# Right-hand weights of the last layer: half of the chunks converted straight into their final buffers, half parked in HBM

## The chip, the cores and the metric

One Trainium2 chip, one core. The time is device microseconds of one execution, the median over runs. Engines: PE is TensorE, DVE is VectorE, ACT is ScalarE, POOL is GpSimd, SP is SyncE, which issues nearly all transfers of this kernel.

## The reference

Windowed attention (4 batches, 8 heads, 576 positions, window 64, scaled scores, softmax) gives `x` of 2304 x 512. Then two MLPs of width 2048:

```python
h = x @ w_in
g = np.maximum(h, 0.0) + alpha * np.minimum(h, 0.0)
x = (g @ w_out).astype(np.float32)
...
h = x @ w_in
g = h * (1.0 / (1.0 + np.exp(-h)))
return (g @ w_out).astype(np.float32)
```

The weights of the second MLP are `w_in2` and `w_out2`. All weights come as 64-bit floats.

## The kernel before, in words

The 2304 tokens are 6 tiles of 384. The kernel runs in four layers: attention with the first product of MLP 1, the second product of MLP 1 ("layer 2"), the first of MLP 2 ("layer 3") and the second of MLP 2 ("layer 4"). Layers 2 to 4 do each 2 x 2 block product with seven products in place of eight (a Winograd form of Strassen's scheme), so each needs seven combinations of left sides and seven of right sides. For precision an operand is split into a high part, which ScalarE casts to `fp32r` (line 339), and a remainder, which VectorE subtracts (line 340); `parts` does the cast at once and puts the remainder on the list `lows`, and `rests` issues these at the next step. Three matmuls (high by high, high by remainder, remainder by high) make one product.

Layer 3 has `NU` = 3 thirds (pairs of token tiles, `u`) of `KH` = 8 units each (chunks of 128 columns, `c`), and `unit(u, c, ...)` runs seven products of six matmuls (line 572) in the order B11, T3, B21, T2, T4, B22 of the unit before, T1. After a product ScalarE copies a bank (`fork`, line 577, tile `fk`), VectorE adds (`blend`, line 582, tile `c`), ScalarE applies SiLU and SP stores the tile to HBM (`finish`, lines 587 and 589, tiles `g`). Between two products stands `hook(h)`, h from 0 to 6. It issues the remainders that wait and then whatever the table `plan` holds for `slot(u, c, h) = LAY3 + (u * KH + c) * 7 + h`. `plan` is filled ahead of time: this is where work for layer 4 is placed. `(2, 5, 4)` below stands for slot(2, 5, 4). Everything issued goes to the engines' queues in that order, and each engine takes its queue in order.

Layer 4 has 168 steps `n` (56 for each pair of token tiles); a step is nine matmuls (line 688) on one hidden tile `g` (split by `split_g2`, three steps ahead) and one right side `w`. Hidden tiles come back by `load_g2` (line 643); `sum_g2` makes the left combinations on VectorE (line 663) or by an adding transfer (line 650).

The right sides of layer 4 are made from `w_out2` in 8 chunks of 128 rows and their partners. For a chunk, `park` loads two tiles of 512 KB (`stage`, line 321, tiles `s`, a pool of four buffers), converts 64-bit to 32-bit in three VectorE operations each (`f32_step`, lines 326, 329, 332, tiles `cva`), makes four combinations into one buffer `ts` (`combos`, line 370; the pool `tp` has a single buffer) and writes all seven right sides to HBM (lines 897 to 899, `w_o`). Later `unpark` fetches one right side (128 KB, line 909) and splits it. `job` spreads a chunk's steps evenly from slot w0 to w1 and puts its loads some 9 us ahead, though not before the buffer's last user, which the list `taken` keeps.

Before the change, chunks 0 to 2 are parked in the first third of layer 3 (6 hooks each), 3 to 5 in the second and 6 and 7 in the last (7 each). Of the 56 right sides 37 are fetched in the last third, the other 19 (`late`) in layer 4 from step 12 on, each two steps ahead of its cast. Layer 3's own right sides come in the same way from `w_i`.

Of the kernel before, what the change touches and what calls it, by code (L numbers as in the profile page):

```python
# [8 lines left out]
F32 = mybir.dt.float32  # L9
F32R = mybir.dt.float32r  # L10
# [34 lines left out]
def attention_two_mlps(ctx, tc, q, k, v, w_in1, w_out1, alpha, w_in2, w_out2, out):  # L45
# [43 lines left out]
    def lroom(i, shape, dtype, name):  # L89
        return wroom(HOMES[i % 64], shape, dtype, name)  # L90
# [228 lines left out]
    def stage(src, f):  # L319
        s = stg.tile([P, 2 * DM], U32, name="s64", tag="st")  # L320
        nc.sync.dma_start(out=s, in_=src[f * P:(f + 1) * P, :])
        return s.rearrange("p (f t) -> p f t", t=2)
# [19 lines left out]
    def rests():  # L342
        while lows:
            lows.pop(0)()
# [286 lines left out]
    def load_g2(u, x, c):  # L631
        if u >= NU:
            return
        i, jj, at = {A11: (0, 0, 0), A21: (1, 0, 8), A22: (1, 1, 16), A12: (0, 1, 24)}[x]

        at = (24 - at) if u % 2 and x in (A11, A12) else at
        if u == 0 and x in (A11, A21):

            g = lroom(32 + c if x == A11 else (40, 41, 42, 43, 44, 45, 46, 48)[c], [P, TN], F32, "g")
        else:  # L640
            g = room(at + c, name="g")
        gb[u, x, c] = g
        nc.sync.dma_start(out=g, in_=gd2[2 * u + i, c + KH * jj])

    def sum_g2(u, x, c):
        if u >= NU:
            return

        def add(a, b):
            nc.gpsimd.dma_start(out=gb[u, a, c], in_=gb[u, b, c], accum_op=ALU.add)  # L650
            gb[u, x, c] = gb[u, a, c]
        if x == S4:
            return add(S2, A12)
        if x == S1 and u:
            return add(A21, A22)
        a, b, op = {S3: (A11, A21, ALU.subtract), S1: (A21, A22, ALU.add), S2: (S3, A22, ALU.subtract)}[x]
        if x == S3:
            o = lroom(24 + c if u == 0 and c < 3 else 48 + c, [P, TN], F32, "s3")
        elif u == 0:
            o = room(c if x == S2 else 8 + c, name="s")  # L660
        else:
            o = gb[u, A11, c]
        nc.vector.tensor_tensor(out=o, in0=gb[u, a, c], in1=gb[u, b, c], op=op)
        gb[u, x, c] = o
# [204 lines left out]
    def park(key, c, src, w0, w1):  # L869

        def load(i):
            held.setdefault((key, c), []).append(stage(src, c + i * KH))

        a = {}

        def convert(i, k):
            if k == 0:
                a[i] = cv.tile([P, DM], U32, name="cva", tag="cv")
            f32_step(held[key, c][i], a[i], k)

        def combine(k):
            x, y = (a[i].bitcast(F32) for i in range(2))
            if k == 0:
                a[2] = tp.tile([P, 4, HD], F32, name="ts", tag="ts")
            t = a[2]
            if key == "i2":
                combos(x[:, :HD], y[:, :HD], x[:, HD:], y[:, HD:], t, k)
            else:
                combos(x[:, :HD], x[:, HD:], y[:, :HD], y[:, HD:], t, k, minus=True)
            if k < 3:  # L890
                return
            d = dram.tile([P, 7, HD], F32, name=f"w2_{key}_{c}")
# [12 lines left out]
    def unpark(key, c, v, to):  # L905
# [7 lines left out]
            parts(s[:, 1, :].bitcast(F32), s[:, 0, :], s[:, 1, :])  # L913
        return fetch, split

    def rights3(c, w0, w1):

        for i, v in enumerate(PARKED):
            g = w0 + i * (w1 - w0) // 7
            fetch, split = unpark("i2", c, v, 7 * c + i)  # L920
            at(g - 10, fetch)
            at(g, split)

    def left_sides(u, places, loads_at):
# [6 lines left out]

        taken.extend((places[7], places[9], places[8], places[10]))

    g = -62
    for x in "0 1 a 2 3 b 4 5 c 6 7 d e".split():
        if x.isdigit():
# [8 lines left out]
                      (5, slot(0, 1, 4), slot(0, 3, 1)), (6, slot(0, 3, 1), slot(0, 4, 4)), (7, slot(0, 4, 4), slot(0, 6, 0))):  # L945
        rights3(c, w0, w1)
    left_sides(0, (147, 149, 150, 151, 153, 157, 159, 161, 163, 165, 167), [138, 139, 140, 141])
    g = LAY3 + 9
    for c in range(3):
        park("o2", c, w_out2, g + 6 * c, g + 6 * c + 6)  # L950
    for u in range(NU - 1):
        left_sides(u + 1, [slot(u, c, h) for c, h in ((5, 5), (6, 0), (6, 1), (6, 3), (6, 5), (7, 2), (7, 3), (7, 4), (7, 5), (8, 0), (8, 6))],
                   [slot(u, 4, h) for h in range(3, 7)])
        g = slot(u + 1, 0, 3) + (4 if u == 0 else 6)
        for c in ((3, 4, 5), (6, 7))[u]:
            park("o2", c, w_out2, g, g + 7)
# [3 lines left out]
    order = [m for m in range(7 * KH) if m not in late]  # L960
    order = [m for m in order if m not in (6, 7, 14, 15, 22, 23)]
    order[20:20] = [6, 7, 14, 15, 22, 23]
    for i, m in enumerate(order):
        plan.setdefault(slot(2, 0, 3) + i * 9 // 8, []).append(rights[m][0])
        plan.setdefault(slot(2, 1, 0) + i * 9 // 8, []).append(rights[m][1])

    def hook(g):
        rests()
# [56 lines left out]
    after1.pop(0)()  # L1025
    put_x2()

    for i, c in enumerate(range(KH)):
        at(slot(2, 6, 1) + i * 3 // 4, lambda c=c: load_g2(0, A11, c))
        at(slot(2, 6, 6) + i * 3 // 4, lambda i=i: load_g2(0, A21, i))  # L1030
    for i in range(3):
        if i < 2:
            at(slot(2, 7, 4) + i, lambda i=i: split_g2(i))
        at(slot(2, 7, 2) + i, lambda i=i: sum_g2(0, S3, i))

    prev = None
    for u in range(NU):
# [4 lines left out]
    split_g2(2)  # L1042
    for n in range(NU * STEPS):
        rests()
        if n == 2:
            last_product(prev, stg.tile([P, TN], F32, name="c", tag="st"))
            for c in range(KH):
                load_g2(0, A22, c)
        split_g2(n + 3)
        around2(n)  # L1050
        if n < 5:
            sum_g2(0, S3, 3 + n)
        for i, m in enumerate(late):
            if n == 14 + i * 30 // len(late):
                rights[m][1]()

        if n % KH == 3:
            while ready:
                ready.pop(0)()
        step2(n)  # L1060
        for i, m in enumerate(late):
            if n == 12 + i * 30 // len(late):
                rights[m][0]()


# [45 lines left out]
```

## Time and profile before

| | before |
|---|---|
| median of 3 runs | 835.59 us (834.38 to 836.41) |
| the profiled execution | 840.68 us |
| its span | 838.9 us |
| TensorE busy | 809.0 us (96% of the span) |
| VectorE, ScalarE, GpSimd busy | 631.8, 523.0, 79.9 us |
| granted TensorE clock, mean | 0.994 |
| moved by DMA | 190.47 MB |

Times in the rows below count from the start of the span. A clock of 1.00 is the higher of TensorE's two levels, 2.4 GHz. The chain follows the work that ended last backwards, at each step to what released it; where it says PE for many pieces, nothing else held the end up there. Layer 3 begins at 464.93 us.

### The profile page before, as it was taken

To read this page: it belongs to the slowest core of one execution; us is meant where nothing else is said; L and a number is where in the kernel's file an instruction comes from. 1 tells how busy PE (TensorE), PEld (TensorE's weight loads), DVE (VectorE), ACT (ScalarE), POOL (GpSimd) and SP (SyncE) were. 2 spreads that over 40 slices of the span, in tenths; PEclk is the share of its full clock that TensorE was granted. 3 is DMA by queue.
4 is the path that set the end of the run, shared out by engine and by line. 5 is a ranking of instruction groups with operands and counts; after the bars stand their busy time and mean duration, and the time that the engine had idled before them with its cause. 6 is when DMAs were issued, how large, how long until landed. Compare 5 with 4: busy or idle time off the path is not lost.

```text
span 838.9 us, 17786 instructions
## 1 busy us (share of the span) xinstructions
PE 809.0 (96%) x5976; PEld 786.7 (94%) x5976; DVE 631.8 (75%) x1593; ACT 523.0 (62%) x1381; POOL 79.9 (10%) x108
## 2 busy tenths in 40 slices
PE   5899999999999999999999989999999999999998
PEld 4789999899899999999999989999899999999998
DVE  6897458888988999887889775756664877756754
ACT  6997696676655776554577556546565564554543
POOL 1000000000000033122222000000000020321400
PEclk9999999999999999999999999999999999999999
DMA  8792468788585899999997786784788879659621
GB/s 274 227 312 104 160 197 273 227 291 260 182 290 183 285 212 225 297 227 264 314 240 202 242 313 217 246 304 157 261 271 268 262 167 326 136 120 307 120 59 57
DMA packets 136844, 190.47 MB, mean 227 GB/s; under 512 B 13872, under 2 KB 122928, under 8 KB 136752
## 3 DMA queue, kind: packets, MB, share of 16 engines
q1 hardware_dynamic: 124080, 172.02, 62.4%
q0 software_dynamic: 12672, 17.31, 12.5%
q8 instruction: 47, 0.77, 0.4%
q14 instruction: 45, 0.37, 0.2%
HBM read 110.11 MB, written 61.87 MB: 205 GB/s over the span
## 4 chain that ended last, share of the span: by engine, by line
PE 79%; DMA 9%; DVE 7%; ACT 3%; issue 1%; SPq 1%; ACTq 0%; DVEq 0%
PE acc L688 20%; PE acc L493 19%; PE h L391 18%; PE qa L572 10%; PE qd L572 5%; DMA w<-w_o 3%; PE qb L572 2%; DMA s<-in_moe_w_in_dram 2%; PE pa L293 2%; PE pa L272 2%; PE pa L206 1%; DMA g<-g 1%; DMA kT<-in_k_dram 1%; ACT pr L229 1%; DMA alpha_sb<-in_moe_alpha_dram 1%
## 5 line engine op out<-in xcount | busy, mean ns | idle before, releaser
L391 PE MATMUL h<-x,i 128*128 128x384 f32 x1152 | 210.0, 339 | 2.1 <-DVE i L365 1.2
L391 PEld LDWEIGHTS h<-x,i 128*128 128x128 f32 x1152 | 199.8, 189 | 5.6 <-ACT g L399 2.4
L688 PE MATMUL acc<-w,gh 128*128 128x256 f32 x984 | 145.7, 283 | 0.4 <-ACT gh L339 0.3
L493 PE MATMUL acc<-gh,o 128*128 128x384 f32 x672 | 143.7, 334 | 0.6 <-ACT gh L339 0.6
L688 PEld LDWEIGHTS acc<-w,gh 128*128 128x128 f32 x984 | 130.3, 192 | 1.1 <-ACT gh L339 1.1
L339 ACT CAST gh<-gf 128x384 fp32r<-128x384 f32 x168 | 85.6, 515 | 57.6 <-PE acc L493 48.3
L493 PEld LDWEIGHTS acc<-gh,o 128*128 128x128 f32 x672 | 118.9, 188 | 0.9 <-ACT gh L339 0.9
L572 PE MATMUL qa<-v,w 128*128 128x384 f32 x576 | 110.5, 339 | 5.5 <-ACT fk L577 3.9
L572 PEld LDWEIGHTS qa<-v,w 128*128 128x128 f32 x576 | 101.8, 190 | 7.2 <-ACT fk L577 5.2
L340 DVE TENSOR_TENSOR gl<-gf,gh 128x384 fp32r<-128x384 f32 x168 | 91.7, 557 | 15.8 <-ACT gh L339 12.2
L339 ACT CAST gh<-g 128x384 fp32r<-128x384 f32 x116 | 58.3, 514 | 48.0 <-PE acc L688 46.9
L688 PE MATMUL acc<-w,gl 128*128 128x256 f32 x492 | 86.7, 283 | 0.0
L493 PE MATMUL acc<-gl,o 128*128 128x384 f32 x336 | 86.0, 336 | 0.3 <-DVE gl L340 0.2
L340 DVE TENSOR_TENSOR gl<-g,gh 128x384 fp32r<-128x384 f32 x116 | 62.8, 556 | 29.7 <-ACT gh L339 28.6
L398 ACT ACTIVATE a<-h 128x384 f32<-128x384 f32 x96 | 47.1, 490 | 56.8 <-PE h L391 47.6
L452 POOL DMA_DIRECT2D gf<-gf x48 | 42.0, 909 | 403.6 <-DVE o L340 298.3
L413 DVE SCALAR_TENSOR_TENSOR g<-a,nalpha,g 128x384 f32<-128x384 f32 x96 | 59.0, 615 | 23.3 <-ACT g L399 22.0
L688 PEld LDWEIGHTS acc<-w,gl 128*128 128x128 f32 x492 | 71.3, 192 | 0.0
L340 DVE TENSOR_TENSOR w<-w 128x256 fp32r<-128x256 f32 x112 | 46.7, 422 | 22.6 <-ACT w L339 22.2
L493 PEld LDWEIGHTS acc<-gl,o 128*128 128x128 f32 x336 | 60.2, 188 | 2.3 <-DVE gl L340 2.2
L229 ACT ACTIVATE pr<-pr,nm 128x128 f32<-128x128 f32 x144 | 56.1, 395 | 8.7 <-DVE nm L217 8.7
L339 ACT CAST w<-w 128x256 fp32r<-128x256 f32 x112 | 43.5, 402 | 24.7 <-DMA w<-w_o 20.4
(90 smaller groups left out, 1121.3 us busy)
## 6 DMA issues: line engine op xcount, KB each, us to landing
g<-g SPq DMA_DIRECT2D x192, 192.0 KB, 4.2
gf<-g SPq DMA_DIRECT2D x96, 192.0 KB, 4.2
g<-c SPq DMA_DIRECT2D x96, 192.0 KB, 3.0
s<-in_moe_w_in_dram SPq DMA_DIRECT2D x32, 512.0 KB, 5.9
s<-in_moe_w_out_dram SPq DMA_DIRECT2D x32, 512.0 KB, 5.8
gf<-gf POOLq DMA_DIRECT2D x48, 192.0 KB, 5.3
w<-w_i SPq DMA_DIRECT2D x56, 128.0 KB, 4.1
w<-w_o SPq DMA_DIRECT2D x56, 128.0 KB, 3.3
```

Of the source, the lines that this page charges most:

```text
L229: nc.scalar.activation(out=pr[:, j, :], in_=pr[:, j, :], func=AF.Exp, bias=it[f"nm{hf}"][:, j:j + 1], scale=-1.0, accum_out=it["sm"][:, hf ...
L272: nc.tensor.transpose(pb[:, j * P:(j + 1) * P], it[f"p{hf}"][:, j, :], ident)
L293: nc.tensor.matmul(pb[r, jb * W:(jb + 1) * W], vt[:, jb // 2, r], it[f"pt{hf}"][:, j, side(jb, e)], start=True, stop=True)
L339: nc.scalar.copy(hi, src)
L340: lows.append(lambda: nc.vector.tensor_tensor(out=lo, in0=src, in1=hi.bitcast(F32), op=ALU.subtract))
L391: nc.tensor.matmul(h, w[:, kk, :], x, start=(kk == 0 and n == 0), stop=(kk == KD - 1 and n == 2))
L398: nc.scalar.activation(out=a, in_=h, func=AF.Relu, scale=-1.0)
L413: nc.vector.scalar_tensor_tensor(out=g, in0=a, scalar=nalpha[:, f:f + 1], in1=g, op0=ALU.mult, op1=ALU.add)
L452: nc.gpsimd.dma_start(out=o, in_=g1[u, b, c], accum_op=ALU.add)
L493: nc.tensor.matmul(o[i], w[:, a, i * P:(i + 1) * P], b, start=start and a == 0 and b is gh, stop=c == KH - 1 and b is gl, skip_group_check ...
L572: nc.tensor.matmul(o, w[:, a, k0], b, start=start and kk == 0 and n == 0, stop=kk == 1 and n == 2, skip_group_check=True)
L688: nc.tensor.matmul(acc2[u, v][i], a[:, i * P:(i + 1) * P], w[:, b, :], start=v in (A11, A12, S3) and c == 0 and a is gh and b == 0 and i != 1,
```

## The change

Chunk 0 alone is parked in the first third, over 14 hooks; chunks 1, 2 and 3 in the second, 9 hooks each. Chunks 7, 6, 5 and 4 are no longer parked: `direct` loads, converts and combines them in the last third and splits the seven results straight into the buffers from which layer 4 reads them. These are places that layer 3's own right sides have left by then. Only the 28 right sides of chunks 0 to 3 are fetched: 8 in the last third, 20 in layer 4 from step 5 on, each five steps ahead of its cast. The first tiles of layer 4 (`A11` and `A21`) are loaded in turn from (2, 5, 4) on, and the next ones (`A22`) partly before layer 4 begins. Some tiles get other places.

```diff
-            g = lroom(32 + c if x == A11 else (40, 41, 42, 43, 44, 45, 46, 48)[c], [P, TN], F32, "g")
+            g = lroom(((28, 29, 31, 32, 33, 34, 35, 30) if x == A11 else (40, 39, 36, 41, 38, 42, 37, 43))[c], [P, TN], F32, "g")
...
-            o = lroom(24 + c if u == 0 and c < 3 else 48 + c, [P, TN], F32, "s3")
+            o = lroom((47, 46, 45, 48, 49, 54, 50, 53)[c], [P, TN], F32, "s3")
...
+    def direct(c, w0, w1, to):
+
+        key, a = ("o2", c), {}
+
+        def load(i):
+            held.setdefault(key, []).append(stage(w_out2, c + i * KH))
+
+        def convert(i, k):
+            if k == 0:
+                a[i] = cv.tile([P, DM], U32, name="cva", tag="cv")
+            f32_step(held[key][i], a[i], k)
+
+        def combine(k):
+            x, y = (a[i].bitcast(F32) for i in range(2))
+            if k == 0:
+                a[2] = tp.tile([P, 4, HD], F32, name="ts", tag="ts")
+            combos(x[:, :HD], x[:, HD:], y[:, :HD], y[:, HD:], a[2], k, minus=True)
+
+        def split(i):
+            s = wt["o2", c, PARKED[i]] = lroom(to + i, [P, 2, HD], F32R, "w2")
+            src = a[2][:, i - 3, :] if i > 2 else a[(i + 1) // 2].bitcast(F32)[:, HD * (i == 2):HD * (i == 2) + HD]
+            parts(src, s[:, 0, :], s[:, 1, :])
+        job([lambda: load(0), lambda: load(1)], CONVERT(convert) + [lambda k=k: combine(k) for k in range(4)] +
+            [lambda i=i: split(i) for i in (0, 5, 1, 4, 6, 2, 3)], w0, w1, 6)
...
-    g = LAY3 + 9
-    for c in range(3):
-        park("o2", c, w_out2, g + 6 * c, g + 6 * c + 6)
...
-        g = slot(u + 1, 0, 3) + (4 if u == 0 else 6)
-        for c in ((3, 4, 5), (6, 7))[u]:
-            park("o2", c, w_out2, g, g + 7)
-            g += 7
-    rights = [unpark("o2", m % KH, SEQ[m // KH], 56 + m) for m in range(7 * KH)]
-    late = list(range(4 * KH, 4 * KH + 3)) + list(range(5 * KH, 7 * KH))
...
-        plan.setdefault(slot(2, 0, 3) + i * 9 // 8, []).append(rights[m][0])
-        plan.setdefault(slot(2, 1, 0) + i * 9 // 8, []).append(rights[m][1])
+    park("o2", 0, w_out2, LAY3 + 15, LAY3 + 29)
+    left_sides(1, LEFT(0), [slot(0, 4, h) for h in range(3, 7)])
+    for c in (1, 2, 3):
+        park("o2", c, w_out2, slot(1, 0, 3) + 9 * (c - 1), slot(1, 0, 3) + 9 * c)
+    left_sides(2, LEFT(1), [slot(1, 4, h) for h in range(3, 7)])
+    direct(7, slot(2, 0, 4), slot(2, 1, 6), 56)
+    direct(6, slot(2, 1, 6), slot(2, 3, 0), 0)
+    direct(5, slot(2, 3, 0), slot(2, 4, 2), 7)
+    direct(4, slot(2, 4, 2), slot(2, 5, 4), 14)
+    SPOTS = [63, *range(21, 28), 44, 55, 51, 52, *range(28, 36), *range(36, 44)]
+    rights = [unpark("o2", m % KH, SEQ[m // KH], SPOTS[j]) for j, m in
+              enumerate(KH * k + c for k in range(7) for c in range(4))]
+    for j in range(8):
+        at(slot(2, 4, 6) + 3 * j // 2, rights[j][0])
+        at(slot(2, 5, 6) + 3 * j // 2, rights[j][1])
...
-        at(slot(2, 6, 1) + i * 3 // 4, lambda c=c: load_g2(0, A11, c))
-        at(slot(2, 6, 6) + i * 3 // 4, lambda i=i: load_g2(0, A21, i))
+    for c in range(KH):
+        for x in (A11, A21):
+            at(slot(2, 5, 4) + (2 * c + (x == A21)) * 7 // 8, lambda c=c, x=x: load_g2(0, x, c))
...
-        at(slot(2, 7, 2) + i, lambda i=i: sum_g2(0, S3, i))
+        at(slot(2, 7, 3) + i, lambda i=i: sum_g2(0, S3, i))
+    for c in range(4):
+        at(slot(2, 7, 5) + c // 2, lambda c=c: load_g2(0, A22, c))
...
+        if n < 2:
+            for c in (4 + 2 * n, 5 + 2 * n):
+                load_g2(0, A22, c)
         if n == 2:
             last_product(prev, stg.tile([P, TN], F32, name="c", tag="st"))
-            for c in range(KH):
-                load_g2(0, A22, c)
...
-            if n == 14 + i * 30 // len(late):
-                rights[m][1]()
+        for j in range(8, len(rights)):
+            if n == 10 + (j - 8) * 3 // 2:
+                rights[j][1]()
...
-            if n == 12 + i * 30 // len(late):
-                rights[m][0]()
+        for j in range(8, len(rights)):
+            if n == 5 + (j - 8) * 3 // 2:
+                rights[j][0]()
```

Three places show how the rows move. In them `w_...` are right sides (those split from themselves were fetched), `s_...` the loaded 64-bit tiles, `cva` the converted ones.

The first is VectorE in the first third of layer 3, between the blend of `qd` in unit 2 and the blend of `qb` in unit 3. Before:

```order
L582 TENSOR_TENSOR c<-qd,fk 128x384
L340 TENSOR_TENSOR w_6872<-w_6872 128x256
L332 SCALAR_TENSOR_TENSOR cva<-s_6855,cva 128x512
L370 TENSOR_TENSOR ts<-cva 128x256
L340 TENSOR_TENSOR w_6886<-w_6886 128x256
L370 TENSOR_TENSOR ts<-cva 128x256
L370 TENSOR_TENSOR ts<-ts,cva 128x256
L370 TENSOR_TENSOR ts<-cva,ts 128x256
L582 TENSOR_TENSOR c<-qa,fk 128x384
L340 TENSOR_TENSOR w_6913<-w_6913 128x256
L326 TENSOR_SCALAR cva<-s_6947 128x512
L326 TENSOR_SCALAR cva<-s_6949 128x512
```

Now:

```order
L582 TENSOR_TENSOR c<-qd,fk 128x384
L340 TENSOR_TENSOR w_6868<-w_6868 128x256
L340 TENSOR_TENSOR w_6882<-w_6882 128x256
L329 SCALAR_TENSOR_TENSOR cva<-s_6851,cva 128x512
L332 SCALAR_TENSOR_TENSOR cva<-s_6849,cva 128x512
L582 TENSOR_TENSOR c<-qa,fk 128x384
L340 TENSOR_TENSOR w_6905<-w_6905 128x256
L332 SCALAR_TENSOR_TENSOR cva<-s_6851,cva 128x512
```

The second parked chunk's combinations stood between the two blends, with a third chunk behind; now the only chunk of this third is still being converted there.

The second is VectorE in the last third, around the blend of `qa` in unit 2. Before (the parking of chunk 6 and the remainders of fetched right sides):

```order
L340 TENSOR_TENSOR w_8359<-w_8359 128x256
L370 TENSOR_TENSOR ts<-cva 128x256 x2
L582 TENSOR_TENSOR c<-qa,fk 128x384
L340 TENSOR_TENSOR w_8375<-w_8375 128x256
L370 TENSOR_TENSOR ts<-ts,cva 128x256
L340 TENSOR_TENSOR w_8391<-w_8391 128x256
L370 TENSOR_TENSOR ts<-cva,ts 128x256
L582 TENSOR_TENSOR c<-qb,fk 128x384
```

Now (chunk 6 by `direct`):

```order
L329 SCALAR_TENSOR_TENSOR cva<-s_8253,cva 128x512
L582 TENSOR_TENSOR c<-qa,fk 128x384
L329 SCALAR_TENSOR_TENSOR cva<-s_8284,cva 128x512
L332 SCALAR_TENSOR_TENSOR cva<-s_8253,cva 128x512
L332 SCALAR_TENSOR_TENSOR cva<-s_8284,cva 128x512
L370 TENSOR_TENSOR ts<-cva 128x256
L582 TENSOR_TENSOR c<-qb,fk 128x384
L370 TENSOR_TENSOR ts<-cva 128x256
L370 TENSOR_TENSOR ts<-ts,cva 128x256
L370 TENSOR_TENSOR ts<-cva,ts 128x256
L582 TENSOR_TENSOR c<-qd,fk 128x384
L340 TENSOR_TENSOR w_8444<-cva,w_8444 128x256
```

Conversions now fill every unit of this third, and remainders are taken from `cva` and `ts`, not from fetched tiles.

The third is SP at the end of layer 3, where the first loads of layer 4's hidden tiles stand (`g_0_` are A11, `g_1_` A21; rows of line 589 are stores). Before:

```order
L643 DMA g<-g_0_5_7317 128x384
L589 DMA g_4_13_8922<-c 128x384
L589 DMA g_5_6_8925<-c 128x384
L643 DMA g<-g_0_6_7403 128x384
L643 DMA g<-g_1_0_6841 128x384
L643 DMA g<-g_1_1_6938 128x384
L643 DMA g<-g_0_7_7488 128x384
```

Now:

```order
L909 DMA w_8752<-w_o_3_7873 128x256
L643 DMA g<-g_0_0_6821 128x384
L643 DMA g<-g_1_0_6837 128x384
L589 DMA g_4_12_8775<-c 128x384
L589 DMA g_5_5_8778<-c 128x384
L909 DMA w_8780<-w_o_0_7134 128x256
L643 DMA g<-g_0_1_6902 128x384
```

The first tile of A21 stood behind seven of A11, after the store `g_5_6`; now it follows the first of A11, ahead of the store `g_5_5`.

## Rows read from the trace of the kernel before

**Rows 1.** Windows: length, then busy time (count) of each engine, PEclk, DMA share, GB/s.

```profile
464.93:500.00 35.07, 32.31 (x183) 31.36 (x183) 26.97 (x63) 18.96 (x48) 0.00 (x0) 1.00 0.88 297
500.00:592.00 92.00, 92.00 (x533) 92.00 (x532) 57.62 (x115) 54.62 (x126) 0.00 (x0) 1.00 0.67 235
592.00:620.00 28.00, 25.23 (x134) 24.40 (x133) 20.01 (x48) 15.36 (x41) 0.00 (x0) 0.94 0.85 274
640.00:655.00 15.00, 12.57 (x72) 12.36 (x72) 6.01 (x12) 6.90 (x17) 0.00 (x0) 0.90 0.90 311
```

**Rows 2.** Chain that ended last, in order of time: start, length, piece.

```profile
476.37 3.12 PE qa L572 x18
...
501.82 3.12 PE qa L572 x18
...
589.18 3.12 PE qa L572 x18
...
623.65 3.16 PE qa L572 x18
...
654.50 33.65 PE acc L688 x276
...
703.48 132.03 PE acc L688 x1098
```

**Rows 3.** Waits, 688 to 706 us: engine, line, what for; total, times, longest.

```profile
ACT w L339 <- DMA w<-w_o: 6.6, 5, 2.3
...
PEld acc L688 <- ACT gh L339: 1.1, 3, 0.5
```

**Rows 4.** Timeline, first third: start, length, operation, idle time before and releaser.

```profile
490.15 0.43 DVE L370 TENSOR_TENSOR ts<-cva 128x256 f32<-128x256 f32 x1 [3.90 <-DMA w_o<-ts]
...
492.56 1.32 PE L572 MATMUL qa<-v,w 128*128 128x384 f32 x6 [1.64 <-DVE c L582]
```

**Rows 5.** Timeline, last third.

```profile
601.30 0.41 ACT L339 CAST w<-w 128x256 fp32r<-128x256 f32 x1 [4.64 <-DMA w<-w_o]
...
603.54 1.64 PE L572 MATMUL qa<-v,w 128*128 128x384 f32 x6 [1.87 <-ACT fk L577]
```

**Rows 6.** Timeline, begin of layer 4.

```profile
648.09 1.20 DVE L663 TENSOR_TENSOR s<-g 128x384 f32<-128x384 f32 x2 [3.99 <-DMA g<-g]
...
650.75 1.83 PE L688 MATMUL acc<-w,gs 128*128 128x256 f32 x12 [2.43 <-DVE gs L340]
```

**Rows 7.** Timeline of VectorE: a remainder and a blend, then one parking of the second third.

```profile
499.24 0.42 DVE L340 TENSOR_TENSOR w<-w 128x256 fp32r<-128x256 f32 x1
499.57 0.55 DVE L582 TENSOR_TENSOR c<-qa,fk 128x384 f32<-128x384 f32 x1
...
549.09 0.76 DVE L370 TENSOR_TENSOR ts<-cva 128x256 f32<-128x256 f32 x2 [2.75 <-DMA w_o<-ts]
...
551.03 0.75 DVE L326 TENSOR_SCALAR cva<-s 128x512 uint32<-128x512 uint32 x2
...
553.37 1.29 DVE L332 SCALAR_TENSOR_TENSOR cva<-s,cva 128x512 uint32<-128x512 uint32 x2
554.57 0.55 DVE L582 TENSOR_TENSOR c<-qd,fk 128x384 f32<-128x384 f32 x1
555.04 0.75 DVE L370 TENSOR_TENSOR ts<-cva 128x256 f32<-128x256 f32 x2
...
556.50 0.55 DVE L582 TENSOR_TENSOR c<-qa,fk 128x384 f32<-128x384 f32 x1
```

**Rows 8.** Timeline, units (2, 0) and (2, 1): two loads, a blend, a product.

```profile
584.44 1.32 SPq L321 DMA_DIRECT2D s<-in_moe_w_out_dram  x2
...
589.28 0.56 DVE L582 TENSOR_TENSOR c<-qd,fk 128x384 f32<-128x384 f32 x1 [1.58 <-PE qd L572]
...
594.22 1.20 PE L572 MATMUL qa<-v,w 128*128 128x384 f32 x6
```

**Rows 9.** Tile `s`, 584.3 to 586.2 us: the two loads.

```profile
DMA to landing us min/median/max: 3.7/4.1/4.4
```

More of the change, by code (lines that the diff above doesn't have):

```diff
@@ L932, in left_sides, with LEFT @@
         taken.extend((places[7], places[9], places[8], places[10]))
+    def LEFT(u):
+        return [slot(u, c, h) for c, h in ((5, 5), (6, 0), (6, 1), (6, 3), (6, 5), (7, 2), (7, 3), (7, 4), (7, 5), (8, 0), (8, 6))]
     g = -62
@@ L947, in attention_two_mlps @@
     left_sides(0, (147, 149, 150, 151, 153, 157, 159, 161, 163, 165, 167), [138, 139, 140, 141])
-    g = LAY3 + 9
-    for c in range(3):
-        park("o2", c, w_out2, g + 6 * c, g + 6 * c + 6)
-    for u in range(NU - 1):
-        left_sides(u + 1, [slot(u, c, h) for c, h in ((5, 5), (6, 0), (6, 1), (6, 3), (6, 5), (7, 2), (7, 3), (7, 4), (7, 5), (8, 0), (8, 6))],
-                   [slot(u, 4, h) for h in range(3, 7)])
-        g = slot(u + 1, 0, 3) + (4 if u == 0 else 6)
-        for c in ((3, 4, 5), (6, 7))[u]:
-            park("o2", c, w_out2, g, g + 7)
-            g += 7
-    rights = [unpark("o2", m % KH, SEQ[m // KH], 56 + m) for m in range(7 * KH)]
-    late = list(range(4 * KH, 4 * KH + 3)) + list(range(5 * KH, 7 * KH))
[L960 to L963, printed above, removed]
-        plan.setdefault(slot(2, 0, 3) + i * 9 // 8, []).append(rights[m][0])
-        plan.setdefault(slot(2, 1, 0) + i * 9 // 8, []).append(rights[m][1])
+    park("o2", 0, w_out2, LAY3 + 15, LAY3 + 29)
[13 more added lines that the diff above has]
+        at(slot(2, 5, 6) + 3 * j // 2, rights[j][1])
     def hook(g):
@@ L1026, in attention_two_mlps @@
     put_x2()
-    for i, c in enumerate(range(KH)):
-        at(slot(2, 6, 1) + i * 3 // 4, lambda c=c: load_g2(0, A11, c))
-        at(slot(2, 6, 6) + i * 3 // 4, lambda i=i: load_g2(0, A21, i))
+    for c in range(KH):
+        for x in (A11, A21):
+            at(slot(2, 5, 4) + (2 * c + (x == A21)) * 7 // 8, lambda c=c, x=x: load_g2(0, x, c))
     for i in range(3):
@@ L1052, in attention_two_mlps @@
             sum_g2(0, S3, 3 + n)
-        for i, m in enumerate(late):
-            if n == 14 + i * 30 // len(late):
-                rights[m][1]()
+        for j in range(8, len(rights)):
+            if n == 10 + (j - 8) * 3 // 2:
+                rights[j][1]()
         if n % KH == 3:
@@ L1060, in attention_two_mlps @@
         step2(n)
-        for i, m in enumerate(late):
-            if n == 12 + i * 30 // len(late):
-                rights[m][0]()
+        for j in range(8, len(rights)):
+            if n == 5 + (j - 8) * 3 // 2:
+                rights[j][0]()
 _INS = ["q", "k", "v", "moe_w_in", "moe_w_out", "moe_alpha", "moe2_w_in", "moe2_w_out"]
```

## The prediction

> **What bounds the kernel now.** I read the windows first, cut where the layers meet, because an average over the span hides that TensorE is full in most stretches and short in a few [rows 1]. From 500 to 592 us it is busy all the time; in the other three windows it lacks 2.76, 2.77 and 2.43 us. Idle time alone understates the loss, since a matmul stream that restarts must refill and may find a lower clock (the mean granted clock is 0.94 and 0.90 in two of these three, 1.00 elsewhere). So I read the chain next and measured the loss as lateness against the period [rows 2]. Between 501.82 and 589.18 lie 12 units without a stall: 87.36 / 12 = 7.28 us a unit, 1.04 for each of its 7 products.
>
> - **Stall 1**, first third of layer 3: 476.37 to 501.82 is 25.45 us for three units of 7.28 (21.84). Lost: 3.6 us.
> - **Stall 2**, last third: 589.18 to 623.65 is 34.47 us for four units (29.12). Lost: 5.4 us.
> - **Stall 3**, where layer 4 begins: from 623.65 three units (21.84), then two products (2.08), two steps of layer 4 and one product (1.04). A step of 9 matmuls takes 132.03 x 9 / 1098 = 1.08 us, so this should end at 650.77; the matmuls after it start at 654.50. Lost: 3.7 us.
> - **Stall 4**, in layer 4 near 700 us, where the weight loads waited 1.1 us for a cast [rows 3].
>
> Together 13.8 us. Each has a cause of its own in the timeline. In stall 1 VectorE stands 3.90 us at the first combination of the second parked chunk, since the single `ts` buffer still drains to HBM from the first; a blend behind it comes late, and TensorE waits for that blend [rows 4]. In stall 2 ScalarE stands 4.64 us at a cast whose parked weights have not landed; the fork behind it is late, and TensorE waits 1.87 us for the fork [rows 5]. In stall 3 VectorE stands 3.99 us until the first pair of hidden tiles has landed; their remainder `gs` is late, and TensorE waits 2.43 us [rows 6]. In stall 4 ScalarE waits 6.6 us in five pieces for parked weights [rows 3].
>
> **The change part by part.** TensorE's and GpSimd's sequences keep their operations; the work of the others is moved, and ScalarE has the same number of weight casts (56).
>
> First third: three chunks in 18 hooks become one in 14. There is no second user of `ts` behind the first, so the wait of rows 4 has no place. Minus 3.6. Were the wait kept in part, its cover is the slack worked out below.
>
> Second third: three chunks at 7 hooks become three at 9. Before, VectorE waited 2.75 us here for `ts` too [rows 7], and TensorE was busy 92.00 of 92.00 us [rows 1], so such a wait is hidden. New is that the second load of chunk 1 is issued in hook 0 of the unit and needed in hook 3. A load of this kind was issued at about 585.4 and took 4.4 us [rows 8, 9], so it lands some 5.8 us into its unit, while VectorE gets there some 4.2 us in: 1.6 us of waiting, with the blends behind it. Hidden, cost 0; double that wait and it reaches the edge of the slack.
>
> Last third: 28 of the 56 fetches (128 KB each) and 4 of the 8 parkings (896 KB each) go: 7.3 MB of traffic. Only 8 fetches remain here, in place of 37, issued 7 hooks (7.3 us) ahead of their casts. What the late fetches cost goes: minus 5.4. What comes is VectorE work. In the parking from 551.03 to 556.50 lie its ten operations and two blends; a blend holds the engine 0.47 us (554.57 to 555.04), so converting and combining takes 5.47 - 0.94 = 4.53 us [rows 7]. Seven remainders at 0.33 us (one lasts 0.42, but the next operation starts after 0.33: 499.24 to 499.57) add 2.3. That is 6.8 us a chunk, 27.4 for four; 15 blends in the same 35 hooks add 7.1. Sum 34.5 us of 36.4: VectorE would be 95% taken, and chunk 6, with 8 hooks and 3.4 blends, 6.8 + 1.6 = 8.4 of 8.3. It keeps up, barely.
>
> How late may it be? The blend of `qd` ended at 589.84 and the next product that needs ScalarE's copy of `qa` starts at 594.22 [rows 8]. Between them ScalarE must do a SiLU, the copy, and up to two casts, each some 0.4 to 0.5 us: 1.9 of 4.4, so about 2.5 us of slack. VectorE's lateness I put at 1.2 (two conversions of 0.60 standing ahead of a blend) plus 0.2 (chunk 6) plus 0 to 1.0 (chunk 7's second load landing near 589.8, when VectorE arrives) = 1.4 to 2.4. That lies just inside. Bounds: 0 (nothing here can become faster than the period), and 4.2 (rival 1). I charge 1.0, nearer to 0, because the row with the same kind of work behind a longer wait (2.75) lost nothing.
>
> Layer 4's first loads: they are spread, pair by pair, over the 14 hooks from (2, 5, 4) on, in place of all first tiles from (2, 6, 1) and the second ones behind. The first pair then lands over a unit before its subtraction at (2, 7, 3). Minus 3.7. Four of the next eight loads move ahead of layer 4 as well, behind them on SP; their buffers were last read in the same unit's third product, so SP does not stand. Cost 0.
>
> Late fetches: 20 in place of 19, issued 5 steps (5.4 us) ahead of their casts in place of 2 (2.2 us), and over before the second pair's loads crowd the queue. Minus 1.1.
>
> Sum: -3.6 - 5.4 - 3.7 - 1.1 + 1.0 = -12.8, so 840.68 becomes 827.9. The profiled execution is 5.1 us above the median of 835.59. If those 5.1 lie outside the stalls, the median becomes 822.8; if all of it is longer stalls, 827.9. Stalls that begin with a transfer lie in the first 100 us too, so I give these four about a third of it: -11.1, **824.5 us**.
>
> **The rivals.**
>
> 1. VectorE paces the last third. If an operation held the engine for its whole duration (0.42 for 0.33, 0.69 for 0.60, 0.55 for 0.47: a factor of about 1.2), 34.5 us become 41.4, 5.0 over the 36.4 there are; less 2.5 of slack, 2.5 lost, and 1.7 more if the clock falls as in 592 to 620 (6% of 28 us): 4.2. Then -13.8 + 4.2 + 1.7 (the part not found in the median) = -7.9: 827.7 us. The Trainium skill, VectorE: DVE Perf Modes, Terms (DRAIN), says that after every operation the pipeline is emptied before the next can issue, which is this case. The rows speak against the full factor: the next operation starts 0.07 to 0.09 us before the one ahead ends [rows 7].
> 2. Slower: casts and remainders wait for each other. Each of the 28 splits needs VectorE's combination, then ScalarE's cast, then VectorE again. If VectorE stood for each cast (0.41 [rows 5]), 11.5 us come on top of 5.0: 16.5, less 2.5 is 14.0, and 1.7 of low clock for each chunk makes 20.8. Then -13.8 + 20.8 = +7.0: 842.6 us. It decides from about 4 us of lateness per chunk. Against it: a remainder is issued one hook (1.04 us) after its cast, and stall 2 began with a wait of 4.64, not of 0.4.
> 3. The stalls only move. The loads of chunk 1 and chunk 7 stand behind the left sides' buffers; if they land 2 us later than in rows 9, VectorE is late beyond the slack in both thirds, and stall 1's 3.6 us and half of stall 2 come back: -13.8 + 6.3 + 1.7 = -5.8: 829.8 us.
> 4. The fetches or first tiles still land late, since the traffic of the last 20 us of layer 3 stays dense: 16 tiles of 192 KB and 8 fetches with the stores. Then stalls 3 and 4 stay and the loss of stall 2 is replaced by theirs: about 835, no change.
>
> **How the numbers follow.** Forecast 0.68, rival 1 0.15, rival 2 0.06, rival 3 0.07, rival 4 0.04. The range of 820.5 to 830.0 us has the forecast with its bounds (13.8 kept whole, and a little more, at the low end), rival 1 and rival 3; what is left out is rivals 2 and 4 and the edges. A run of this kernel can tell about 0.2%, 1.7 us. Faster by more than that: 0.68 + 0.15 + 0.07 = 0.90; within it: 0.04; slower: 0.06.
>
> **What would show it.** Right: in the chain, units 7.28 us apart from 465 us to the end of layer 3; no wait of VectorE for `ts` in the first third; no wait of ScalarE for parked weights over 1 us; no wait of VectorE for `g` before layer 4; VectorE near 95% busy between units (2, 0) and (2, 5), with TensorE at 20.00 of 20.00 us. Wrong: TensorE waits for a fork in the last third while VectorE is full (rival 1), while VectorE's idle time is put down to casts (rival 2) or to `w_out` loads (rival 3), or a `DMA` wait before layer 4 (rival 4).

## The result, and the profile after

| | before | after |
|---|---|---|
| median of the runs, us | 836.0 (834.38 to 836.48, 4 runs) | 826.86 (824.28 to 829.71, 4 runs) |
| ratio, 95% interval | | 0.9895 [0.9859, 0.9931] |
| profiled execution, us (span) | 840.68 (838.9) | 827.35 (825.6) |
| TensorE busy, us | 809.0 | 803.1 |
| layers 3 and 4 in the span, us | 838.9 - 464.93 = 373.97 | 825.6 - 463.69 = 361.91 |

The change is faster by 1.05%, some 9 us; 824.5 was forecast and 820.5 to 830.0 was the range. Of the two profiled executions layers 3 and 4 differ by 12.06 us; another 1.24 lie ahead of them, where nothing was changed.

The windows of the changed kernel, cut as in [rows 1] with the last third in pieces (length, busy time and count of TensorE, its weight loads, VectorE, ScalarE and GpSimd, granted clock, DMA share, GB/s):

```profile
463.69:500.00 36.31, 36.31 (x211) 36.31 (x211) 21.83 (x51) 22.64 (x58) 0.00 (x0) 1.00 0.69 225
500.00:580.00 80.00, 80.00 (x463) 80.00 (x462) 50.79 (x100) 45.94 (x105) 0.00 (x0) 1.00 0.66 224
...
590.00:600.00 10.00, 9.24 (x54) 8.92 (x53) 9.54 (x23) 6.09 (x16) 0.00 (x0) 1.00 0.60 188
600.00:610.00 10.00, 9.73 (x56) 9.41 (x55) 9.97 (x25) 6.13 (x16) 0.00 (x0) 1.00 0.76 267
610.00:620.00 10.00, 10.00 (x59) 9.79 (x58) 9.84 (x25) 7.20 (x19) 0.00 (x0) 1.00 0.40 142
...
640.00:655.00 15.00, 15.00 (x124) 15.00 (x124) 13.45 (x30) 9.63 (x22) 0.00 (x0) 1.00 1.02 343
```

TensorE is full in the first third and where layer 4 begins, and the granted clock is 1.00 in all these windows (in the kernel before 0.94 and 0.90 in two of them [rows 1]). It lacks 1.03 us, between 590 and 610, and there VectorE is busy 9.5 to 10 of 10 us.

The chain that ended last (start, length, piece), which answers to [rows 2]:

```profile
475.13 3.12 PE qa L572 x18
...
569.77 3.12 PE qa L572 x18
...
580.94 6.67 DMA s<-in_moe_w_out_dram
...
589.90 3.36 DMA s<-in_moe_w_out_dram
...
607.77 3.12 PE qa L572 x18
615.25 3.12 PE qa L572 x18
622.53 3.12 PE qa L572 x18
629.81 3.12 PE qa L572 x18
...
637.09 2.08 PE qa L572 x12
...
642.36 179.83 PE acc L688 x1494
```

From 475.13 to 569.77 lie 13 units: 94.64 / 13 = 7.28, no stall. From 569.77 to 607.77 five units take 38.00 in place of 36.40 and the next takes 7.48: 1.8 us late. Then the period holds, and layer 4 is one piece to its end. The chain names the load that began the delay, at 580.94. (The load at 589.90 stands on the chain ahead of a blend at 593.26; the timeline shows no wait of VectorE in front of that blend.) The timeline (start, length, operation, idle time before and releaser) shows the load's issue, VectorE's wait for it, a pair of left-side remainders of layer 3 behind it, and two waits of TensorE for a fork of ScalarE. Its first row is the same kind of wait in the second third, which cost TensorE nothing:

```profile
527.92 0.43 DVE L326 TENSOR_SCALAR cva<-s 128x512 uint32<-128x512 uint32 x1 [2.27 <-DMA s<-in_moe_w_out_dram]
...
580.94 0.44 SPq L321 DMA_DIRECT2D s<-in_moe_w_out_dram  x1
...
587.64 0.43 DVE L326 TENSOR_SCALAR cva<-s 128x512 uint32<-128x512 uint32 x1 [2.32 <-DMA s<-in_moe_w_out_dram]
...
590.86 1.02 DVE L340 TENSOR_TENSOR v<-xq,v 128x384 fp32r<-128x384 f32 x2
...
593.42 2.35 PE L572 MATMUL qa<-v,w 128*128 128x384 f32 x12 [0.76 <-ACT fk L577]
...
605.40 0.79 PE L572 MATMUL qa<-v,w 128*128 128x384 f32 x3 [0.27 <-ACT fk L577]
```

The load is chunk 7's second one; it took 6.7 us to land. That is no rare value: in layer 3 of the kernel before (tile `s`, 460 to 640 us) the sixteen loads of this kind landed after

```profile
DMA to landing us min/median/max: 3.5/5.0/7.3
```

The waits from the start of layer 3 on (engine, line, what for; total, times, longest) show what became of the old ones:

```profile
DVE w L340 <- ACT w L339: 8.8, 9, 1.4
...
DVE cva L326 <- DMA s<-in_moe_w_out_dram: 5.8, 4, 2.3
...
PE qa L572 <- ACT fk L577: 1.0, 2, 0.8
...
DVE ts L370 <- DMA w_o<-ts: 0.4, 1, 0.4
ACT w L339 <- DMA w<-w_o: 0.4, 1, 0.4
```

VectorE's wait of 3.90 us for `ts` [rows 4] is 0.4 at most, ScalarE's 4.64 for parked weights [rows 5] and the 6.6 near 700 us [rows 3] are 0.4 together, and VectorE's wait for `g` [rows 6] is not in the list.

### The profile page after: what moved, and what is told of

Read it like the earlier page. It is cut to its first block, busy times and chain, and to the rows that moved or that the text cites. A ratio compares the mean times of both kernels' runs of the same rounds, so it can differ in the third digit from the quotient of the medians.

```text
span 825.6 us, 17722 instructions
## 1 busy us (share of the span) xinstructions
PE 803.1 (97%) x5976; PEld 784.1 (95%) x5976; DVE 631.1 (76%) x1593; ACT 523.4 (63%) x1381; POOL 79.9 (10%) x108
## 4 chain that ended last, share of the span: by engine, by line
PE 80%; DVE 8%; DMA 7%; ACT 3%; issue 1%; SPq 1%; ACTq 0%; DVEq 0%
PE acc L688 22%; PE h L391 18%; PE acc L493 18%; PE qa L572 10%; PE qd L572 5%; PE qb L572 3%; DMA s<-in_moe_w_out_dram 2%; DMA s<-in_moe_w_in_dram 2%; PE pa L293 2%; PE pa L272 1%; DMA gf<-g 1%; DMA w<-w_i 1%; PE pa L206 1%; DVE pr L217 1%; DVE g L413 1%
## 5 line engine op out<-in xcount | busy, mean ns | idle before, releaser
L572 PE MATMUL qa<-v,w 128*128 128x384 f32 x576 | 108.4, 335 | 1.0 <-ACT fk L577 1.0
L572 PE MATMUL qd<-v,w 128*128 128x384 f32 x288 | 57.7, 334 | 0.0
L572 PEld LDWEIGHTS qd<-v,w 128*128 128x128 f32 x288 | 50.6, 188 | 0.0
```

What stands on the lines that cost most here:

```text
L572: nc.tensor.matmul(o, w[:, a, k0], b, start=start and kk == 0 and n == 0, stop=kk == 1 and n == 2, skip_group_check=True)
```

## The experiments

All twelve runs in one table, with the two kernels. Lateness is read from each run's profiled execution: in layer 3 from the distances of the chain's x18 rows against 7.28 us a unit; in layer 4 from its x12 row to the end of TensorE's last piece, less the 184.54 us of run e4, the shortest (634.69 to 639.96 + 179.27). Where the chain has no x12 row, it is put a whole number of units behind the last x18 row; for the kernel before, 623.65 + 3 x 7.28. Each run has one profiled execution, so the lateness is that of one execution and the median that of several. Ratios are each run's to the kernel before on its own chip.

| run | what differs | ratio [95%] | median us | late, first third | last third | layer 4 |
|---|---|---|---|---|---|---|
| before | | 1 | | 3.6 | 5.4 | 5.5 |
| after | the change | 0.9895 [0.9859, 0.9931] | 826.86 | 0 | 1.8 | 0.6 |
| e0 | the change, again | 0.9891 [0.9876, 0.9906] | 827.59 | 0 | 1.8 | 0.9 |
| e1 | first third as before | 0.9922 [0.9905, 0.9939] | 829.73 | 4.9 | 1.5 | 0.7 |
| e2 | first tiles as before | 0.9909 [0.9892, 0.9925] | 828.93 | 0 | 2.0 | 4.2 |
| e3 | fetch lead 2 as before | 0.9896 [0.9874, 0.9918] | 827.54 | 0 | 1.6 | 1.9 |
| e4 | direct: later, 9 hooks each | 0.9861 [0.9847, 0.9876] | 824.75 | 0 | 0 | 0 |
| e5 | direct: later, 7 hooks each | 0.9882 [0.9861, 0.9903] | 826.36 | 0 | 2.1 | 0.3 |
| e8 | direct: chunk 7 alone later | 0.9892 [0.9873, 0.9912] | 827.54 | 0 | 1.2 | 2.1 |
| e9 | direct: same start, 10 hooks | 0.9861 [0.9841, 0.9881] | 824.85 | 0 | 0.3 | 0.1 |
| e6 | before + free buffer for `ts` | 0.9949 [0.993, 0.9969] | 833.04 | 0 | 5.6 | 3.1 |
| e7 | before + direct | 1.0006 [0.9988, 1.0025] | 837.28 | 3.9 | 1.8 | 9.5 |
| e10 | e4, lead 2 | 0.9863 [0.9833, 0.9893] | 825.26 | 0 | 0 | 1.8 |
| e11 | e4, first tiles as before | 0.9881 [0.9855, 0.9907] | 827.2 | 0 | 0 | 3.9 |

**e0, the yardstick.**

> The changed kernel once more, as the yardstick for the runs beside it. Expected: 0.9895 of the kernel before (0.986 to 0.993); in the profile layers 3 and 4 take about 361.9 us, with one stall of about 1.8 us in the last third of layer 3.

It came out so: 9.1 us below the kernel before (7.9 to 10.4), and the same single stall.

### What is left: a late load, or a full VectorE? (e4, e5, e8, e9)

The changed kernel has `direct` for chunk 7 from slot (2, 0, 4) to (2, 1, 6), then chunks 6, 5, 4 with 8, 9 and 9 hooks. e4:

```diff
-    direct(7, slot(2, 0, 4), slot(2, 1, 6), 56)
-    direct(6, slot(2, 1, 6), slot(2, 3, 0), 0)
+    direct(7, slot(2, 1, 0), slot(2, 2, 2), 56)
+    direct(6, slot(2, 2, 2), slot(2, 3, 4), 0)
...
```

> The changed kernel, but the four chunks that are converted in the last third start 3 hooks (3.1 us) later and have 9 hooks each, so that chunk 7's loads, whose place is set by the buffers that come free, stand further ahead of their use, and the last third's VectorE work is spread over 38 hooks in place of 35. My theory (the 1.8 us that are left come from VectorE standing 2.3 us for chunk 7's second load and then having no idle time to catch up in): that wait goes, units of 7.28 us to the end of layer 3, 1.8 us below the changed kernel (0.9895 - 0.0021 = 0.987). Rival (VectorE is full whatever the load does, and the lateness comes from its own work): the last third stays 1 to 2 us late, no change. A third way: the later splits push into the begin of layer 4, with a wait of TensorE for weights there, 1 to 3 us above the changed kernel.

e5:

```diff
+    direct(7, slot(2, 1, 0), slot(2, 2, 0), 56)
+    direct(6, slot(2, 2, 0), slot(2, 3, 0), 0)
...
```

> The changed kernel, but the four chunks that are converted in the last third start 3 hooks later and have 7 hooks each, 28 in place of 35. If VectorE's work sets the pace of the last third once it is full: 6.8 us of a chunk and three blends of 0.47 are 8.2 us in 7.28, 0.95 too much for each of four chunks, 3.8 in all, less 2.5 of slack: late by 1.3 us or somewhat more at the end, with TensorE waiting for forks. My theory for the 1.8 us that are left in the changed kernel (a load that lands late) takes the same work off them, since the loads now land in time: about -0.5 us against the changed kernel, and +2 against the version with 9 hooks. Rival (a full VectorE is hidden, only the load counted): as with 9 hooks, 2.8 us below the changed kernel.

e8:

```diff
+    direct(7, slot(2, 0, 6), slot(2, 1, 6), 56)
...
```

> The changed kernel, but chunk 7 alone starts 2 hooks (2.1 us) later and ends where it ended, 7 hooks in place of 9; the other three chunks stay. If the load's lateness is the cause of the 1.8 us: VectorE's wait of 2.3 us for it goes down to about 0.2, and the 1.8 go with it, although VectorE's work is denser: about 825, 0.9980 of the changed kernel. If the density of VectorE's work is the cause: 8.2 us in 7.28, 0.9 late in chunk 7 and no idle time behind it to make it good: 1.8 us as before, or up to 1 more.

e9:

```diff
+    direct(7, slot(2, 0, 4), slot(2, 2, 0), 56)
+    direct(6, slot(2, 2, 0), slot(2, 3, 3), 0)
...
```

> The changed kernel, with the same start of chunk 7 (so its second load is late as there), but 10 hooks for each chunk in place of 8.75. If the load's lateness alone is the cause: VectorE waits about 2.3 us as before, TensorE waits about 0.8 us for the fork behind it, and most of the 1.8 us stays (1 to 1.8). If the density is the cause, since VectorE can't make the wait good: the 2.3 us are made good in chunk 7 and 6, TensorE waits 0 to 0.8 us, and 1 to 1.8 us of the 1.8 go.

e4 has no stall in layers 3 and 4, VectorE waits for none of the last third's loads, and it is 2.8 us below e0 by the medians (0.30% by the ratios). It changed the start and, by one hook in 35, the spacing; the other three are to tell which counts. e9 keeps the start. Its timeline and its chain:

```profile
586.94 0.43 DVE L326 TENSOR_SCALAR cva<-s 128x512 uint32<-128x512 uint32 x1 [2.15 <-DMA s<-in_moe_w_out_dram]
```

```profile
591.09 3.12 PE qa L572 x18
598.64 3.12 PE qa L572 x18
605.92 3.12 PE qa L572 x18
```

VectorE waits nearly as long for the same load (2.15 against 2.32 us), and TensorE loses 0.27 (7.55 against 7.28) in place of 1.8. e5 is the reverse: no wait for that load, but 28 hooks for the work of 35. Its chain:

```profile
599.18 3.12 PE qa L572 x18
606.58 3.13 PE qa L572 x18
...
614.85 3.13 PE qa L572 x18
...
623.13 3.12 PE qa L572 x18
630.41 3.12 PE qa L572 x18
```

The lost time comes in equal steps, units of 8.27 and 8.28 us, while VectorE is busy 9.9 of every 10: there its work is the pace, and the rival of e5, that a full VectorE is hidden, falls. Of the two cases set out for e9 the second came: the room in VectorE's queue decides what the wait costs, 0.3 us with 10 hooks and 1.8 with 8.75; and the second third of the changed kernel hides a wait of 2.27 us while VectorE is busy 50.79 of 80.00 us. But e4 has nearly the spacing of the change, 9 hooks each against 9, 8, 9 and 9, with the load in time, and loses nothing. So neither the load nor the density is the cause by itself: the late load starts the delay, the missing room keeps it, and taking away either was enough. No run has the load in time at exactly the change's spacing. e8 did not do what it was for: the first conversion still stood behind the same blend, VectorE waited 1.89 us all the same, 1.2 us were lost in layer 3 and 2.1 at the begin of layer 4. Its time is that of the change, and by itself it decides nothing.

### Stall 1 (e1, e6)

e1, to the changed kernel:

```diff
-    park("o2", 0, w_out2, LAY3 + 15, LAY3 + 29)
+    for c in range(3):
+        park("o2", c, w_out2, LAY3 + 9 + 6 * c, LAY3 + 15 + 6 * c)
-    for c in (1, 2, 3):
-        park("o2", c, w_out2, slot(1, 0, 3) + 9 * (c - 1), slot(1, 0, 3) + 9 * c)
+    park("o2", 3, w_out2, slot(1, 0, 3) + 18, slot(1, 0, 3) + 27)
```

> The changed kernel, but its first third parks three chunks at 6 hooks each, as before. My theory (stall 1 comes from the second parked chunk's combinations, which need the single `ts` buffer while the first chunk's store still drains): VectorE waits about 3.9 us for `ts` again, the three units from the first one on are 3.6 us late, and the time is 3.6 us above the changed kernel (0.9895 + 0.0043 = 0.994). Rival (the stall came from something else that the change took away, such as the traffic of later fetches): VectorE waits little, TensorE stays at the 7.28 us period, 0 to 1 us above the changed kernel.

e6, to the kernel before (`Pair` is two tiles of free room, each stored by itself):

```diff
-                a[2] = tp.tile([P, 4, HD], F32, name="ts", tag="ts")
+                a[2] = tp.tile([P, 4, HD], F32, name="ts", tag="ts") if (key, c) != ("o2", 1) else Pair(
+                    lroom(56 + i, [P, 2, HD], F32, "tw") for i in range(2))
...
```

> The kernel before, but the second chunk that is parked in the first third makes its combinations in two tiles of free room instead of the single `ts` buffer, with one store more. My theory (stall 1 is VectorE's wait for `ts` while the first chunk's store drains): the wait of 3.90 us at the first combination is gone, and with it up to 3.6 us: 832.5 to 834. Rival (the fetches of layer 3's weights that land late there, since three parkings in 18 hooks fill the queues, would stop TensorE by themselves): the wait for `ts` goes, TensorE still stands, and the time stays at that of the kernel before.

e1 puts the wait back. Its list of waits, and its chain:

```profile
DVE ts L370 <- DMA w_o<-ts: 5.0, 1, 5.0
```

```profile
473.20 3.12 PE qa L572 x18
...
480.48 3.12 PE qa L572 x18
...
499.97 3.12 PE qa L572 x18
```

From 473.20 to 499.97 are 26.77 us for three units: 4.9 late, and 2.6 us slower than e0 by the ratios. e6 takes the shared buffer from the kernel before, at the price of one store more, and the stall is gone, 15 units in 109.20:

```profile
472.10 3.12 PE qa L572 x18
...
581.30 3.12 PE qa L572 x18
...
597.58 3.13 PE qa L572 x18
...
616.02 3.13 PE qa L572 x18
```

4.2 us faster than before (2.6 to 5.9), with the three parkings still in 18 hooks. So the cause is the single buffer, not the traffic: shown by both directions. The last two rows show stall 2 untouched (34.72 us for four units, 5.6 late).

### Stalls 3 and 4 (e2, e11; e3, e10)

e2, to the changed kernel, and e11, to e4:

```diff
-    for c in range(KH):
-        for x in (A11, A21):
-            at(slot(2, 5, 4) + (2 * c + (x == A21)) * 7 // 8, lambda c=c, x=x: load_g2(0, x, c))
+    for i, c in enumerate(range(KH)):
+        at(slot(2, 6, 1) + i * 3 // 4, lambda c=c: load_g2(0, A11, c))
+        at(slot(2, 6, 6) + i * 3 // 4, lambda i=i: load_g2(0, A21, i))
```

> The changed kernel, but the first tiles of layer 4 are loaded as before: all first tiles from the seventh product of the last unit on, all second ones behind them; the subtractions stay where the change put them. My theory (stall 3 is the order and the lateness of these loads): VectorE waits some 3 to 4 us for the first pair, layer 4 begins 3.7 us late, the time is 3.7 us above the changed kernel (0.994). Rival (the loads were late because 37 fetches and 4 stores more ran through the same queues in the last third, which are gone): the pair lands in time, 0 to 1 us above the changed kernel (0.990).

> The version with 9 hooks for each directly converted chunk, starting 3 hooks later (824.75, spread 0.7), but the first tiles of layer 4 loaded as before. By stall 3 in the profile of the kernel before: 3.7 us above that version (828.4). By the run on the changed kernel (+1.4 in the median, though its profile lost 4.2 at that place): about 826.2. Rival (with the last third on time, layer 4 begins earlier against its loads): more than 3.7 above.

e3, to the changed kernel, and e10, to e4 (the fetches):

```diff
-            if n == 5 + (j - 8) * 3 // 2:
+            if n == 8 + (j - 8) * 3 // 2:
```

> The changed kernel, but the late fetches of layer 4 are issued 2 steps ahead of their casts, as before, in place of 5; the casts stay where they are. My theory (stall 4 comes from the short lead): ScalarE waits some 6 us in pieces for parked weights near 700 us and TensorE about 1.1 us for it, 1.1 us above the changed kernel. Rival (it came from the second pair's loads that crowd the queue, and the casts are now over before them): 0 to 0.3 us above the changed kernel.

> The version with 9 hooks for each directly converted chunk, starting 3 hooks later (824.75, spread 0.7), but the late fetches 2 steps ahead of their casts, as before, in place of 5. If the short lead costs TensorE 1.1 us (stall 4), this shows against that version: about 825.8, with waits of ScalarE for parked weights of some 6 us and a loss near 685 us. Rival (ScalarE's waits are hidden in part): 824.75 to 825.2.

With the old loads, stall 3 is back where it was, though the last third's traffic is gone: the rival of e2, that the pair lands in time, falls. The timeline of e2, then of e11:

```profile
639.32 0.56 DVE L663 TENSOR_TENSOR s<-g 128x384 f32<-128x384 f32 x1 [4.17 <-DMA g<-g]
...
641.33 1.01 PE L688 MATMUL acc<-w,gs 128*128 128x256 f32 x3 [2.63 <-DVE gs L340]
```

```profile
640.82 1.70 PE L688 MATMUL acc<-w,gs 128*128 128x256 f32 x12 [3.21 <-DVE gs L340]
```

But the runs pay less for it than these two profiled executions: e2 1.5 us over e0 by the ratios, e11 1.7 over e4 (2.5 by the medians), against 3.3 and 3.9 in layer 4. My 3.7 for e2 was too much, and its rival's 0 to 1 too little. That the stall's size differs from execution to execution is likely (in e6, whose loads are those of the kernel before, layer 4 is 3.1 late in place of 5.5), but the executions without a profile do not show theirs.

With the short lead ScalarE's waits for parked weights are back, in e3 (first row) and in e10 (second), of the lists of waits:

```profile
ACT w L339 <- DMA w<-w_o: 6.3, 4, 2.6
```

```profile
ACT w L339 <- DMA w<-w_o: 5.6, 5, 1.9
```

Layer 4 is 1.0 and 1.8 us later in these executions, but the medians differ by 0 and 0.5 us, within the spread. That the lead is worth something stays likely and unproven.

### The last third alone (e7)

The kernel before with `direct`, its four parked chunks and the new places of the tiles; the late fetches are:

```diff
+        for j in range(8, len(rights)):
+            if n == 14 + (j - 8) * 3 // 2:
+                rights[j][1]()
...
+        for j in range(8, len(rights)):
+            if n == 12 + (j - 8) * 3 // 2:
+                rights[j][0]()
```

> The kernel before with the direct conversion of four chunks in the last third alone: the first third, the order and place of layer 4's first loads, and the lead of the late fetches are as before. If the parts add up, the gain of the last third is what the leave-one-out runs have not explained: of 9.0 us between the two kernels about 2.5 belong to the first third, 1.4 to the first loads and 0 to 0.5 to the lead, so 4.6 to 5.1 below the kernel before (about 831.5); by my terms -5.4 + 1.8 = -3.6 (832.5). Rival (stalls 1 and 3 grow where the last third is on time, or shrink, since they share its queues): outside 829.5 to 834.

Both sums fell, since nothing is gained, and the rival came: 837.28 lies outside its 829.5 to 834, and stall 3 grew. In the last third e7 does what the change does (1.8 us late in place of 5.4, 3.6 gained), and layer 4 gives it back (9.5 in place of 5.5). TensorE's waits in the timeline of e7, and the piece of its chain behind the begin of layer 4:

```profile
489.38 1.34 PE L572 MATMUL qa<-v,w 128*128 128x384 f32 x6 [1.57 <-DVE c L582]
...
595.45 2.38 PE L572 MATMUL qa<-v,w 128*128 128x384 f32 x12 [0.78 <-ACT fk L577]
...
645.51 2.93 PE L688 MATMUL acc<-w,gs 128*128 128x256 f32 x12 [3.61 <-DVE gs L340]
...
669.49 0.62 PE L688 MATMUL acc<-w,gh 128*128 128x256 f32 x3 [0.88 <-DVE w L340]
```

```profile
650.36 17.15 PE acc L688 x139
```

These rows divide the 4.0 us. The piece at 650.36 answers to the one at 654.50 in [rows 2]: by the prediction's sum for stall 3 (from 631.83 + 7.28 = 639.11 in place of 645.49) it starts 5.97 us late in place of 3.73, so 2.2 are a longer stall 3 (3.61 against 2.43 [rows 6]; behind the wait the granted clock is 0.50, the lower level, from 646 to 650 us, where TensorE had been busy 0.49 of the 4.00 us before). Around the row at 669.49 two steps take 3.48 us, from 666.82 to 670.30, in place of 2.16: 1.3 more. The rest, 0.4, lies near 700 us. Why stall 3 is longer here is not shown.

The row at 669.49 is new: TensorE waits for a weight tile's remainder itself, which it does nowhere in layer 4 of the kernel before. A likely reason can be read in the code. Before, the late fetches were the last groups of products alone; where four chunks are parked and only 8 fetches are left in layer 3, the third group's weights are late ones too. They are for steps 16 to 19, and e7 casts them in steps 14, 15, 17 and 18, so only one or two steps ahead; the change casts them from step 10 on. VectorE has no room to help here, busy 10.00 of 10.00 us from 660 to 670, so the remainder stands behind other work; no run moves the casts alone.

## Why the prediction was right, and where it was off

- **Four stalls, four causes: held for three, likely for the fourth.** The four waits are gone in the changed kernel; a new one leaves 1.8 us in the last third. Undone one at a time, stall 1 (e1, and e6 from the other side) and stall 3 (e2, e11) come back at their old places with their old waits. Stall 2 goes where the last third alone is changed (e7, 5.4 to 1.8). For stall 4 the wait comes back, a cost in the medians is not shown.
- **Second third, cost 0: held.** VectorE waited 3.5 us for loads there (5.8 less chunk 7's 2.3), 2.27 of them at one load, for which 1.6 was estimated, and TensorE is busy 80.00 of 80.00 us.
- **VectorE "keeps up, barely": nearly.** The price of a chunk held: 6.8 us and three blends gave 8.2 us, and e5 measured 8.27 a unit where VectorE sets the pace. But the sum for the last third left out the two left-side remainders at 590.86, which hold VectorE 0.9 us: 35.4 of 36.4 us, not 34.5, and from 590 to 620 it was busy 29.35 of 30.00. e5 was 2.1 us late in place of 1.3, so the slack behind VectorE was 4 x 0.99 - 2.1 = 1.9 us, not 2.5.
- **Rival 1** is a real mechanism (e5) but not at its price: by whole durations, a factor of 1.2, such a unit would take 9.8 us, and it took 8.27. The Trainium skill, VectorE: DVE Perf Modes, Terms (DRAIN), has the pipeline emptied before the next operation issues; the measured unit does not show that as a cost on top of the starts in [rows 7].
- **The failed size in the last third: "I charge 1.0".** The profiled execution lost 1.8 in the last third and 0.6 in layer 4. The assumed landing, 4.4 us from [rows 9], was 6.7, so VectorE stood 2.3 us and not 0 to 1.0: 1.4 + 2.3 = 3.7 of lateness against 2.5 of slack gives 1.2, with the two remainders 2.1; 1.8 was measured. I took one landing time, from another place, for a load whose lateness had a price, where the same trace had 3.5 to 7.3 us. And the row that drew my 1.0 towards 0, a wait of 2.75 us that lost nothing, stood in a stretch where VectorE was busy 57.62 of 92.00 us [rows 1]: it says nothing of a full VectorE. e9 corrects this account in part: the same wait cost 0.3 us where the work had 10 hooks, so the missing room belongs to the cause as much as the load.
- **Stall 4, "minus 1.1"**, was the wrong price for an edit that does more. I priced the new lead as if the late fetches were the same tiles as before; they now hold the third group's weights too, and e7, which casts them from step 14 on, waited for them at 669.49. The lead alone was worth 0 to 0.5 us in the medians (e3, e10), within the spread. And the terms do not simply add: e7, with the gain of the last third, lost it again, 2.2 of 4.0 us by a longer stall 3 and 1.3 around the wait at 669.49.
- **The other rivals did not come, but for a sign of rival 3.** Rival 2: VectorE's longest wait for a cast of weights is 1.4 us, and the list has nine of them, 8.8 us in layers 3 and 4. Rival 3: its sign came, a late load of chunk 7 with TensorE waiting for a fork, and with it two signs of a right forecast failed, the even units and the full TensorE in the last third; but it cost 1.8 us, not 8.0, since chunk 1's wait stayed hidden and stall 1 did not return. Rival 4: VectorE does not wait for first tiles, and ScalarE waits 0.4 us for parked weights; one wait of ScalarE for a hidden tile, 2.27 us at 646.83, leaves TensorE full.
- **The step from the profiled execution to the median failed by size.** I gave "about a third" of the 5.1 us by which the profiled execution lay above the median to these four stalls: 11.1 us. Layers 3 and 4 differ by 12.06 in the two profiled executions (12.8 forecast; 14.5 late before, of which I had listed 13.8, and 2.4 after), and the runs by 9.1. If the changed kernel's profiled execution is a usual one there (e0's layers 3 and 4 took 362.2), about 3.0 of the 5.1, three fifths, were longer stalls. The rest fits what lies ahead of them: layer 3 begins at 464.93 us in that execution, the latest of the fourteen traces, and at 462.7 in the mean of the others. Stall 3 points the same way: 3.7 us in that execution, 1.5 to 2.5 in medians. These two, 0.7 and 1.3 us, are the 2.0 us by which the gain was put too high; 0.4 more is the kernel before, 836.0 in place of 835.59.

The two versions e4 and e9 beat both kernels: 824.75 and 824.85 us, 0.9861 of the kernel before, about 2.5 us below the change, with the same number of instructions on every engine and 9 or 10 hooks for each directly converted chunk.

## What to carry to other kernels

Find each stall's own wait before costing a change, and size it from several executions: the lateness in one profiled execution was about twice what the runs paid in e1 (4.9 against 2.6) and e2 (3.3 against 1.5), while in e6 the runs gained more than the stall in the profile (4.2 against 3.6). For a transfer that something waits for, take the spread of all its kind in the trace, not one row. And add up every operation of the engine in the stretch. A VectorE filled to 95% and more hid its work behind a full TensorE only as long as nothing in it waited; 10 hooks a chunk in place of 8.75 with the wait kept (e9) were worth more than 7 with the wait gone (e5). And when tiles are moved from a store into direct conversion, check which of the remaining transfers are now the late ones, and whether their casts still come ahead of the product that needs them.

## What the runs showed of the hardware that was not expected

- Of two 512-KB loads issued 1.4 us apart at about 580 us, the second landed after 6.7 us in the changed kernel, 6.7 in e0, 6.5 in e9. The pair in [rows 9] took at most 4.4, the sixteen of layer 3 in the same trace 3.5 to 7.3.
- Where layer 3 begins differs between executions whose code up to there is the same: 460.66 us in e6, 464.93 in the kernel before. A profiled time must be compared from such a mark on, not from zero.
